# Weight gradients finished inside the second batch's tail, sums read from PSUM, and convolution gradients written as rows

## Chip, cores and metric

The kernel runs on one core of one Trainium2 chip. The metric is the device time of one execution in microseconds (us), as the median of several runs. Engines: PE is TensorE (matmul), PEld its weight load, DVE is VectorE, ACT is ScalarE, POOL is GpSimd, SP is SyncE; "SPq" and "ACTq" are DMA issues by SyncE and ScalarE.

## The reference, cut to what matters

The reference is the forward pass of one branch-merging encoder layer and all of its gradients, for 2 batches of 4000 tokens of width D = 144, in bfloat16. The kernel returns the output, the gradient of `x`, and seven weight gradients (out2 to out8). Convolutions have K = 5 taps.

```python
def _fwd_reference(x, w_qkv, w_att_out, w_mlp_in, dw_csgu, w_mlp_out, dw_merge, w_merge):
    xa = _layernorm(x)
    q, k, v = split(xa @ w_qkv)
    glob = softmax(q k^T * D**-0.5) v @ w_att_out
    u, g = split(gelu(layernorm(x) @ w_mlp_in)); g = _layernorm(g)
    gc = sum over i of shift(g, i) * dw_csgu[i]          # dw_csgu is (5, 144)
    m = concat(glob, (u * gc) @ w_mlp_out)
    m = m + sum over i of shift(m, i) * dw_merge[i]      # dw_merge is (5, 288)
    return x + m @ w_merge

def reference(*args, grad_out):                          # shortened
    out, vjp = jax.vjp(_fwd_reference, *args)
    return (out, *vjp(grad_out))
```

Weight gradients are sums over the tokens of both batches. out5 is the gradient of `dw_csgu` and out7 that of `dw_merge`: five rows each, with the channels along the row.

## The kernel before

For each batch the program runs a head, an attention phase and a *tail*. The tail walks over 32 token blocks in 16 half-steps plus 4, and gathers two sets of sums in PSUM: `EF` (correlations of activations with the shifted `grad_out`, 12 tiles of 144 columns) and, in the four last half-steps, `gr`. At the end of a tail both are spilled to DRAM:

```python
        def spill_ef():
            EFs = pp.tile([128, 12, D], F32, name="EFs")
            nc.gpsimd.memset(EFs[64:128, 10:12, :], 0.0)
            for n_ in range(3):
                nc.scalar.copy(EFs[:, n_ * 3:n_ * 3 + 3, :], EF[:, n_, 0:3 * D].rearrange("p (a b) -> p a b", b=D))
            # ... two more copies ...
            nc.sync.dma_start(k.A.EF_d[b][:], EFs[:])
        # spill_gr() does the same with gr, to k.A.gr_d[b]

            for h in range(NPR + 4):                  # NPR = 16
                # ... loads, turns, EF matmuls, dx matmuls of this half-step, cut ...
                if h == NPR:
                    spill_ef()
                # ...
                if 0 <= h - 4 < NPR:
                    out_mm(h - 4)                     # the output's matmuls
                if h >= NPR:
                    gr_part(range((h - NPR) * 8, (h - NPR) * 8 + 8))
                # ...
            spill_gr()
```

After both batches, `finish_weights` loads weights and both batches' sums, adds them, and works out the weight gradients:

```python
def finish_weights(k, W):
    # ...
        for name, (dr, shp) in W.fin.items():
            F[name] = fp.tile(shp, BF, name="f_" + name)
            nc.sync.dma_start(F[name][:], dr[:])
        # ...
        for t, dr, n in ((A.EF, A.EF_d, 12), (A.gr, A.gr_d, 4)):
            o = fp.tile([128, n, D], F32, name="f_o%d" % n)
            nc.sync.dma_start(t[:], dr[0][:])
            nc.sync.dma_start(o[:], dr[1][:])
            nc.vector.tensor_tensor(t[:], t[:], o[:], op=ALU.add)
        # ... ET, E80: the sums as bf16 ...
        for kk in range(5):                           # 16 partitions of each tap, to partition 0
            nc.sync.dma_start(ETr[0:DR, :, kk, :], E80[(4 - kk) * DR:(5 - kk) * DR, :, :])
        # dU: 8 PSUM tiles of matmul, 20 pairs of VectorE operations
        for h in range(2):
            for ct in range(2):
                for (k0, k1) in ((0, 3), (3, 5)):
                    # ... pt = WmT^T (ET, ETr) ...
                    for kk in range(k0, k1):
                        nc.vector.scalar_tensor_tensor(dU[0:cw, h, ct, :], pt[0:cw, kk - k0, :], W.wm[...], dU[0:cw, h, ct, :], op0=ALU.mult, op1=ALU.add)
                        nc.vector.scalar_tensor_tensor(jk[0:cw, :], pt[0:cw, kk - k0, :], 1.0, W.UT[h][0:cw, ct, :], op0=ALU.mult, op1=ALU.mult, accum_out=dwm[...])
        # the turn: ET and ETr transposed to Ej; dm: 20 VectorE operations, to out8
        # transposes and small products, to out2, out3, out4, out6
        # ...
        with nc.allow_non_contiguous_dma(reason="small conv weight gradients"):
            nc.sync.dma_start(k.out5[:, 0:128].rearrange("k c -> c k"), dwcb[:, 0, :])
            nc.sync.dma_start(k.out5[:, 128:D].rearrange("k c -> c k"), dwcb[112:128, 1, :])
            for h in range(2):
                nc.sync.dma_start(k.out7[:, h * D:h * D + 128].rearrange("k c -> c k"), dwmb[:, h, 0, :])
                nc.sync.dma_start(k.out7[:, h * D + 128:h * D + D].rearrange("k c -> c k"), dwmb[0:DR, h, 1, :])
```

In the program's text the writes of `dwcb` (out5) stand at the end. They depend on nothing late, so the scheduler moved them forward.

Of the kernel before, what the change touches and what calls it, by code (L numbers as in the profile page):

```python
# [10 lines left out]
ALU = mybir.AluOpType  # L11
# [1866 lines left out]
def phase_tail(k, W, b, S):  # L1878
# [3 lines left out]
    with ExitStack() as es:  # L1882
# [13 lines left out]
        EF = ps_e.tile([128, 4, 512], F32, tag="EF", name="EF")  # L1896
# [40 lines left out]
        def corr(g, j):  # L1937
            i = g * 4 + j
            for s in range(6):
                lhs = G["gs", g][:, j, s, 0:128] if s < 5 else G["g80", g][:, j, :]  # L1940
                mw = 128 if s < 5 else 80
                for h, mv in enumerate((S.Yn[:, i, :], G["ug", g][:, j, :])):
                    q = s * 2 + h
                    nc.tensor.matmul(EF[0:mw, q // 3, (q % 3) * D:(q % 3 + 1) * D], lhs, mv,
                                     start=(i == 0 and q % 3 == 0), stop=(i == NBK - 1), skip_group_check=True)
# [76 lines left out]
        def spill_ef():  # L2022
            EFs = pp.tile([128, 12, D], F32, name="EFs")
            nc.gpsimd.memset(EFs[64:128, 10:12, :], 0.0)
            for n_ in range(3):
                nc.scalar.copy(EFs[:, n_ * 3:n_ * 3 + 3, :], EF[:, n_, 0:3 * D].rearrange("p (a b) -> p a b", b=D))
            nc.scalar.copy(EFs[:, 9:10, :], EF[:, 3, 0:D].rearrange("p (a b) -> p a b", b=D))
            nc.scalar.copy(EFs[0:80, 10:12, :], EF[0:80, 3, D:3 * D].rearrange("p (a b) -> p a b", b=D))
            nc.sync.dma_start(k.A.EF_d[b][:], EFs[:])

        def gr_part(r):
            if r[0] == 0:
                st["gr"] = ps_e.tile([128, 4, 512], F32, tag="EF", name="gr")
            gr = st["gr"]
            for i in r:
                for n_, (p_, w) in enumerate(parts(i)):
                    nc.tensor.matmul(gr[0:w, n_ // 2, (n_ % 2) * D:(n_ % 2 + 1) * D], p_, S.xaa[:, i, :],  # L2037
                                     start=(i == 0 and n_ % 2 == 0), stop=(i == NBK - 1), skip_group_check=True)

        def spill_gr():  # L2040
            gr = st.pop("gr")
            grs = pp.tile([128, 4, D], F32, name="grs")
            nc.gpsimd.memset(grs[:, 3, :], 0.0)
            nc.scalar.copy(grs[:, 0:2, :], gr[:, 0, 0:2 * D].rearrange("p (a b) -> p a b", b=D))
            nc.scalar.copy(grs[:, 2, :], gr[:, 1, 0:D])
            nc.scalar.copy(grs[0:48, 3, :], gr[0:48, 1, D:2 * D])
            nc.sync.dma_start(k.A.gr_d[b][:], grs[:])

        NPR = NBK // 2
        with tc.manual_schedule():  # L2050
# [3 lines left out]
            prep(0)  # L2054
            for h in range(NPR + 4):
# [28 lines left out]
                if h >= NPR:  # L2084
                    gr_part(range((h - NPR) * 8, (h - NPR) * 8 + 8))
                if h < NPR:
# [8 lines left out]
def finish_weights(k, W):  # L2095
    nc, tc = k.nc, k.tc
    A = k.A
    c = float(D) ** -0.5
    with tc.tile_pool(name="fw", bufs=1) as fp, tc.tile_pool(name="fw_ps", bufs=3, space=PSUM) as ps:
        id_ = W.ident  # L2100
# [4 lines left out]
        W.WoT, W.UT, W.U, W.WmT, W.Wqkv = F["WoT"], [F["UT0"], F["UT1"]], [F["U0"], F["U1"]], F["WmT"], F["Wqkv"]  # L2105
        A.EF = fp.tile([128, 12, D], F32, name="f_EF")
        A.gr = fp.tile([128, 4, D], F32, name="f_gr")
        for t, dr, n in ((A.EF, A.EF_d, 12), (A.gr, A.gr_d, 4)):
            o = fp.tile([128, n, D], F32, name="f_o%d" % n)
            nc.sync.dma_start(t[:], dr[0][:])  # L2110
            nc.sync.dma_start(o[:], dr[1][:])
            nc.vector.tensor_tensor(t[:], t[:], o[:], op=ALU.add)

        ET = fp.tile([128, 2, 5, D], BF, name="f_ET")
        E80 = fp.tile([128, 2, D], BF, name="f_E80")
        for h in range(2):
            for kk in range(5):
                nc.vector.tensor_copy(ET[:, h, kk, :], A.EF[:, (4 - kk) * 2 + h, :])
            nc.scalar.copy(E80[0:80, h, :], A.EF[0:80, 10 + h, :])
        ETr = fp.tile([128, 2, 5, D], BF, name="f_ETr")  # L2120
        nc.gpsimd.memset(ETr[:], 0.0)
        for kk in range(5):
            nc.sync.dma_start(ETr[0:DR, :, kk, :], E80[(4 - kk) * DR:(5 - kk) * DR, :, :])
        dU = fp.tile([128, 2, 2, D], F32, name="f_dU")
        nc.vector.memset(dU[:], 0.0)
        dwm = fp.tile([128, 2, 2, 5], F32, name="f_dwm")
        nc.vector.memset(dwm[:], 0.0)
        jk = fp.tile([128, D], F32, name="f_jk")
        for h in range(2):
            for ct in range(2):  # L2130
                cw = 128 if ct == 0 else DR
                for (k0, k1) in ((0, 3), (3, 5)):
                    n = (k1 - k0) * D
                    pt = ps.tile([128, 3, D], F32, tag="H")
                    for kt, e_ in enumerate((ET, ETr)):
                        nc.tensor.matmul(pt[0:cw, 0:k1 - k0, :].rearrange("p a b -> p (a b)"), W.WmT[:, h, kt, ct * 128:ct * 128 + cw],  # L2136
                                         e_[:, h, k0:k1, :].rearrange("p a b -> p (a b)"), start=(kt == 0), stop=(kt == 1))
                    for kk in range(k0, k1):
                        nc.vector.scalar_tensor_tensor(dU[0:cw, h, ct, :], pt[0:cw, kk - k0, :], W.wm[0:cw, h, ct, kk:kk + 1], dU[0:cw, h, ct, :], op0=ALU.mult, op1=ALU.add)  # L2139
                        nc.vector.scalar_tensor_tensor(jk[0:cw, :], pt[0:cw, kk - k0, :], 1.0, W.UT[h][0:cw, ct, :], op0=ALU.mult, op1=ALU.mult, accum_out=dwm[0:cw, h, ct, kk:kk + 1])  # L2140

        for h in range(2):
            Ej = fp.tile([128, 2, 5, D], BF, name="f_Ej%d" % h)
            nc.gpsimd.memset(Ej[:, 1, :, :], 0.0)
            for kk in range(5):
                for jt_ in range(2):
                    jw = 128 if jt_ == 0 else DR
                    pt = ps.tile([128, D], BF, tag="T")
                    nc.tensor.transpose(pt[0:jw, 0:128], ET[:, h, kk, jt_ * 128:jt_ * 128 + jw], id_[:])  # L2149
                    nc.tensor.transpose(pt[0:jw, 128:D], ETr[0:DR, h, kk, jt_ * 128:jt_ * 128 + jw], id_[0:DR, 0:DR])  # L2150
                    nc.scalar.copy(Ej[0:jw, jt_, kk, :], pt[0:jw, :])
            for ct in range(2):
                cw = 128 if ct == 0 else DR
                dm = fp.tile([128, D], F32, name="f_dm%d%d" % (h, ct))
                nc.vector.memset(dm[:], 0.0)
                for (k0, k1) in ((0, 3), (3, 5)):
                    pt = ps.tile([128, 3, D], F32, tag="H")
                    for kt in range(2):
                        nc.tensor.matmul(pt[0:cw, 0:k1 - k0, :].rearrange("p a b -> p (a b)"), W.U[h][:, kt, ct * 128:ct * 128 + cw],  # L2159
                                         Ej[:, kt, k0:k1, :].rearrange("p a b -> p (a b)"), start=(kt == 0), stop=(kt == 1))  # L2160
                    for kk in range(k0, k1):
                        nc.vector.scalar_tensor_tensor(dm[0:cw, :], pt[0:cw, kk - k0, :], W.wm[0:cw, h, ct, kk:kk + 1], dm[0:cw, :], op0=ALU.mult, op1=ALU.add)  # L2162
                dmb = fp.tile([128, D], BF, name="f_dmb%d%d" % (h, ct))
                nc.vector.tensor_copy(dmb[0:cw, :], dm[0:cw, :])
                nc.sync.dma_start(k.out8[h * D + ct * 128:h * D + ct * 128 + cw, :], dmb[0:cw, :])

        def tr(src, R, C, name):

            nk, nck = (R + 127) // 128, (C + 127) // 128
            t = fp.tile([128, nck, R], BF, name=name)  # L2170
            nc.vector.memset(t[:], 0.0)
            for cc in range(nck):
                w = min(128, C - cc * 128)
                for kt in range(nk):
                    rk = min(128, R - kt * 128)
                    pt = ps.tile([128, D], BF, tag="T")
                    nc.tensor.transpose(pt[0:w, 0:rk], src[0:rk, kt, cc * 128:cc * 128 + w], id_[0:rk, 0:rk])
                    nc.vector.tensor_copy(t[0:w, cc, kt * 128:kt * 128 + rk], pt[0:w, 0:rk])
            return t

        def prod_out(lhs_k, rhs_k, rc0, scale, out_ap, name):
            for mt in range(2):
                mw = 128 if mt == 0 else DR
                pt = ps.tile([128, 3, D], F32, tag="H")
                for kt in range(2):
# [132 lines left out]
```

## Time and profile before

| | before |
|---|---|
| median, us | 1449.94 (3 runs, 1448.42 to 1453.59) |
| span of the profiled run, us | 1449.8 |
| start of the second tail, us | 1281.7 |
| first `gr` matmul of the second tail | 1361.8 |
| last `gr` matmul ends | 1374.6 |

The table of windows of the kernel before gives each engine's busy us in a stretch (number of instructions in brackets), then the granted TensorE clock, the DMA engines' busy share and GB/s:

```profile
core 0: us, PE busy (x) PEld busy (x) DVE busy (x) ACT busy (x) POOL busy (x), PEclk, DMA share, GB/s
1340.00:1350.00 10.00, 9.72 (x157) 9.54 (x157) 5.76 (x22) 5.59 (x15) 6.06 (x13) 1.00 0.72 185
...
1380.00:1390.00 10.00, 1.06 (x4) 0.32 (x4) 4.22 (x14) 0.52 (x2) 0.00 (x0) 0.50 0.68 243
1390.00:1400.00 10.00, 1.08 (x5) 0.46 (x5) 0.65 (x3) 0.29 (x2) 0.00 (x0) 0.50 0.02 4
1400.00:1410.00 10.00, 9.67 (x46) 4.10 (x45) 6.69 (x38) 4.86 (x19) 0.00 (x0) 0.50 0.01 2
```

From 1340 to 1350 us TensorE is busy 97% of the time (from 1350 to the last `gr` 89%). After the last `gr` the engines work in turns for 75 us, at half clock from 1380. From 1390 to 1400 us almost nothing works, and the DMA engines are idle too (share 0.02). The chain of waits of the kernel before (start, length, what) says why:

```profile
1379.03 6.89 DMA f_o<-EF_d
1386.02 1.97 DVE f_EF L2112
1388.01 0.53 ACT f_E L2119 x2
1388.60 10.72 DMA f_ETr<-f_E
1401.06 0.93 PE pt L2136 x2
...
1425.66 0.50 ACT f_dWk_o L2188 x2
```

The sums come back from DRAM (6.9 us), are added and cast, and then five copies of 9 KB each wait 10.7 us. The timeline of SyncE in the kernel before shows what stood ahead of them, and what was issued last:

```profile
1380.79 0.43 SPq L2226 DMA_DIRECT2D out_dram<-f_dwcb  x1
1381.27 0.54 SPq L2227 DMA_DIRECT2D out_dram<-f_dwcb  x1
1388.60 3.18 SPq L2123 DMA_DIRECT2D f_ETr<-f_E  x5
...
1429.27 0.42 SPq L2229 DMA_DIRECT2D out_dram<-f_dwmb  x1
1429.73 4.15 SPq L2230 DMA_DIRECT2D out_dram<-f_dwmb  x1
```

Its DMA issues (count, KB each, median us from issue to landing):

```profile
f_ETr<-f_E SPq DMA_DIRECT2D x5, 9.0 KB, 10.7
...
out_dram<-f_dwi SPq DMA_DIRECT2D x1, 72.0 KB, 1.6
...
out_dram<-f_dwmb SPq DMA_DIRECT2D x2, 1.2 KB, 16.7
```

A store of 72 KB in rows lands in 1.6 us; one of 1.2 KB in columns takes 16.7. Two such column writes (`f_dwcb`) were issued over 7 us ahead of the `f_ETr` copies, and the last ones (`f_dwmb`) end the program.

### The profile page before, as it was taken

The page shows a single profiled execution, that of the slowest core. Times are in us where ns is not written, and L with a number is a line of the kernel's source. Part 1 is how long each engine was busy: PE and PEld are TensorE (multiplying, and loading weights), DVE is VectorE, ACT ScalarE, POOL GpSimd, SP SyncE. Part 2 cuts the span into 40 slices and gives each one's busy share as a digit, 9 for nine tenths or more (in the row PEclk, how much of TensorE's full clock was granted, in tenths as well). Part 3 has the DMA queues.
Part 4 walks back from the last instruction along what each step waited for, and adds up shares of the span by engine and source line. Part 5 has one row for each costly group of instructions (what it writes and reads, how often), then busy time and mean ns, then how long its engine had stood idle before and what let it go on. Part 6 is the DMA issues. An engine that isn't in the chain of part 4 may idle for free. (4 is left out here: it accounts for less than half of the span.)

```text
span 1449.8 us, 40173 instructions
## 1 busy us (share of the span) xinstructions
PE 1289.7 (89%) x15366; PEld 981.9 (68%) x15366; DVE 933.5 (64%) x3213; ACT 807.8 (56%) x2377; POOL 544.5 (38%) x937
## 2 busy tenths in 40 slices
PE   5989999999999998899679999999999999979832
PEld 2727777777676776789553777777776777679811
DVE  5537778688677776355335778777767777636442
ACT  3746666666666754254365667666666665435310
POOL 2224435444434432355232343453434343245300
PEclk9969999999999999899896999999999999999955
DMA  4439999899999989756525999998987989966520
GB/s 135 121 60 158 162 169 173 152 187 160 163 167 163 164 176 175 169 164 171 177 76 102 156 183 143 177 176 148 186 168 148 160 149 192 176 158 187 138 84 13
DMA packets 652288, 220.65 MB, mean 152 GB/s; under 512 B 589876, under 2 KB 649012, under 8 KB 652084
## 3 DMA queue, kind: packets, MB, share of 16 engines
q1 hardware_dynamic: 651220, 217.89, 76.7%
q8 instruction: 122, 2.00, 0.6%
q14 instruction: 82, 0.67, 0.2%
q10 hardware_dynamic: 864, 0.09, 0.1%
HBM read 58.00 MB, written 25.13 MB: 57 GB/s over the span
## 5 line engine op out<-in xcount | busy, mean ns | idle before, releaser
L1778 DVE SCALAR_TENSOR_TENSOR Sm<-pD,Pm 128x500 bf16<-128x500 f32 x512 | 326.3, 675 | 226.6 <-ACT Pm L1777 185.4
L1777 ACT ACTIVATE Pm<-pS 128x500 bf16<-128x500 f32 x512 | 296.0, 585 | 110.6 <-PE pS L1772 107.0
L1831 PE MATMUL X<-Qs,Sm 128*128 128x144 bf16 x2048 | 293.6, 227 | 4.4 <-DVE acc L1842 4.4
L1832 PE MATMUL X<-Bt,Pm 128*128 128x144 bf16 x2048 | 293.7, 227 | 0.0
L1840 POOL TENSOR_TENSOR acc<-xs,acc 128x432 f32<-128x432 f32 x160 | 179.0, 1119 | 242.6 <-ACT xs L1839 242.2
L1832 PEld LDWEIGHTS <-Pm 128*128 128x128 bf16 x2048 | 201.3, 98 | 15.5 <-issue 5.2
L1831 PEld LDWEIGHTS <-Sm 128*128 128x128 bf16 x2048 | 201.5, 98 | 10.4 <-issue 0.3
L1839 ACT COPY xs<-X 128x432 f32<-128x432 f32 x160 | 83.1, 519 | 170.7 <-PE X L1832 166.6
L1772 PE MATMUL pS<-xaT,QTm 128*128 128x500 bf16 x512 | 160.6, 397 | 0.0
L1811 PE MATMUL y<-xaa,PT 128*128 128x144 bf16 x2048 | 149.4, 226 | 9.1 <-DVE B_t L1819 8.9
L1772 PE MATMUL pD<-xaT,BTm 128*128 128x500 bf16 x512 | 157.5, 390 | 0.0
L1811 PE MATMUL y<-xaa,ST 128*128 128x144 bf16 x2048 | 148.8, 226 | 0.0
L1811 PEld LDWEIGHTS <-PT 128*128 128x128 bf16 x2048 | 134.4, 98 | 19.8 <-issue 13.8
L1811 PEld LDWEIGHTS <-ST 128*128 128x128 bf16 x2048 | 133.3, 98 | 9.5
L1842 DVE TENSOR_TENSOR acc<-X,acc 128x432 f32<-128x432 f32 x192 | 110.6, 576 | 28.4 <-PE X L1832 28.0
L1768 PE MATMUL pD<-XR,QBr 16*128 16x500 bf16 x512 | 119.2, 393 | 4.6 <-DVE Sm L1778 4.2
L1800 POOL TENSOR_SCALAR nr<-nd,rl 128x1 f32<-128x1 f32 x64 | 22.6, 353 | 258.5 <-DVE nd L1794 258.5
L1768 PE MATMUL pS<-XR,QBr 16*128 16x500 bf16 x512 | 110.6, 395 | 1.7 <-ACT QBr L1755 1.4
L1777 ACT ACTIVATION_READ_ACCUMULATOR Pm<-pS 128x1 f32 x512 | 103.3, 202 | 0.0
L1772 PEld LDWEIGHTS <-BTm 128*128 128x128 bf16 x512 | 51.9, 101 | 64.3 <-issue 9.8
L1772 PEld LDWEIGHTS <-QTm 128*128 128x128 bf16 x512 | 29.3, 98 | 80.7 <-issue 80.7
L2008 POOL TENSOR_SCALAR cc<-xaa,n 128x144 f32<-128x144 bf16 x64 | 36.0, 570 | 70.0 <-DVE n L2005 56.7
(584 smaller groups left out, 2602.1 us busy)
## 6 DMA issues: line engine op xcount, KB each, us to landing
gs<-in_grad_out_dram SPq DMA_DIRECT2D x24, 720.0 KB
gtap<-gn_d SPq DMA_DIRECT2D x16, 720.0 KB
dh_d<-dh SPq DMA_DIRECT2D x32, 144.0 KB, 2.8
dhr<-dh_d SPq DMA_DIRECT2D x16, 288.0 KB, 4.1
gs<-in_grad_out_dram SPq DMA_DIRECT2D x8, 540.0 KB
xg<-in_x_dram SPq DMA_DIRECT2D x28, 144.0 KB, 4.2
dug_d<-dug SPq DMA_DIRECT2D x16, 144.0 KB, 1.8
gn_d<-gn_t SPq DMA_DIRECT2D x32, 72.0 KB, 2.9
```

Of the source, the lines that this page charges most:

```text
L1768: nc.tensor.matmul(o_[:, 0:SC], QBr[rr, bi, :], S.XR[rr, c2, 0:SC], start=True, stop=False)
L1772: nc.tensor.matmul(p_[h][:, 0:SC], w_[:, bi, :], S.xaT[:, c0 + h * SC:c0 + (h + 1) * SC], start=False, stop=True)
L1777: nc.scalar.activation(P[:, pb, c1:c1 + SC], pS[h][:, 0:SC], ACT.Exp, accum_out=ld8[:, 0, n:n + 1])
L1778: nc.vector.scalar_tensor_tensor(Sm[:, pb, c1:c1 + SC], pD[h][:, 0:SC], 1.0, P[:, pb, c1:c1 + SC], op0=ALU.mult, op1=ALU.mult, accum_out=l ...
L1800: nc.gpsimd.tensor_scalar(nr[:], nd[:], rl[:], 1.0, op0=ALU.mult, op1=ALU.mult)
L1811: nc.tensor.matmul(y[:, w, :], src[:, jj, :], S.xaa[:, j, :], start=(j == 0), stop=(j == NBK - 1))
L1831: nc.tensor.matmul(X[:, jj, :], Sm[:, i % NP, j * 128:(j + 1) * 128], Qs[:, i % 4, :], start=(kk == 0 and jj == 0), stop=False, skip_group ...
L1832: nc.tensor.matmul(X[:, jj, :], P[:, i % NP, j * 128:(j + 1) * 128], Bt[:, i % 4, :], start=False, stop=(kk == 1), skip_group_check=True)
L1839: nc.scalar.copy(xs[:, 0:nj, :], X[:, 0:nj, :])
L1840: nc.gpsimd.tensor_tensor(a_, xs[:, 0:nj, :], a_, op=ALU.add)
L1842: nc.vector.tensor_tensor(a_, X[:, 0:nj, :], a_, op=ALU.add)
L2008: nc.gpsimd.tensor_scalar(cc[:, q, :], S.xaa[:, 2 * p + q, :], n[:, 1, q:q + 1], n[:, 0, q:q + 1], op0=ALU.mult, op1=ALU.add)
```

## The change

It has four parts.

1. Weights and the first batch's sums are loaded at the start of the second tail, with the fills of the tiles that need zeros.
2. The second batch's sums are not spilled: VectorE adds them to the first batch's straight from PSUM. Four separate EF banks let `gr` start when two are free.
3. The arithmetic of the weight gradients is put in four *slots* in the four last half-steps, one behind each `gr_part`; the rest follows in `gr()`.
4. out5 and out7 are transposed on TensorE and leave as contiguous rows. Some small stores go out on ScalarE's queue.

```diff
-        EF = ps_e.tile([128, 4, 512], F32, tag="EF", name="EF")
+        EF = [ps_e.tile([128, 512], F32, tag="EF%d" % n, name="EF") for n in range(4)]
+        fin_ = Finish(k, W, es, ps_t, ps_e) if b else None
@@ spill_ef
+            if fin_:
+                return fin_.ef(EF)
@@ the tail's loop
             prep(0)
+            if fin_:
+                fin_.loads()
             for h in range(NPR + 4):
@@
                 if h >= NPR:
                     gr_part(range((h - NPR) * 8, (h - NPR) * 8 + 8))
+                    if fin_:
+                        fin_.step(h - NPR)
@@
-def finish_weights(k, W):
+class Finish:
+    def loads(self):
+        # ... weights, EF0, gr0 from DRAM ...
+        nc.gpsimd.memset(self.Wk32[:], 0.0)
+        nc.gpsimd.memset(self.ETr[:], 0.0)
+        for h in range(2):
+            nc.gpsimd.memset(self.Ej[h][:, 1, :, :], 0.0)
+        nc.gpsimd.memset(self.dU[:], 0.0)
+        nc.gpsimd.memset(self.dwm[:], 0.0)
+        nc.gpsimd.tensor_copy(dwcb[:], A.dwc[:])
+        pt = self.T()
+        nc.tensor.transpose(pt[0:10, 0:128], dwcb[:].rearrange("p a b -> p (a b)"), W.ident[:])
+        nc.scalar.copy(o[0:10, :], pt[0:10, 0:128])
+        nc.sync.dma_start(self.k.out5[:, 0:128], o[0:5, :])
+        nc.sync.dma_start(self.k.out5[:, 128:D], o[5:10, 112:128])
+    def ef(self, EF):
+        # ... five tensor_tensor adds ET = EF (PSUM) + EF0 ...
+        for m in range(5):
+            nc.sync.dma_start(self.ETr[0:DR, :, m, :], ET[m * DR:(m + 1) * DR, 10:12, :])
+    def step(self, n):
+        if n == 0:
+            self.turn(0)
+            self.turn(1)
+        elif n == 1:
+            self.dU_part(0, 0)
+            self.dU_part(0, 1)
+        elif n == 2:
+            self.dU_part(1, 0)
+            self.dU_part(1, 1)
+        else:
+            # ... dwm transposed, out7 as rows; out6, dWv, dWo ...
+    def gr(self, gr):
+        # ... gb = gr (PSUM) + gr0; dWq, dWk, out4 ...
+        for h in range(2):
+            for ct in range(2):
+                self.dm_part(h, ct)                   # out8
```

(All of it cut to its core; the computation of each gradient is the one of before.)

## The prediction

> **What bounds the kernel now.** Until 1374 us it is held by TensorE (table of windows: 1310 to 1350 us, PE 9.7 to 9.9 of 10 us busy). The change touches what follows: the last `gr` matmul starts at 1374.3 us (timeline), the span is 1449.8, so 75 us are a serial epilogue with granted clock 0.5 from 1380. The chain of waits and the timeline split it:
> - to 1386.0: SyncE issues loads, `f_o<-EF_d` lands.
> - to 1388.6: sum in SBUF (1.97 us), casts.
> - to 1399.3: `f_ETr<-f_E`, 10.7 us for five 9 KB copies. I blame the queue ahead: the element-wise `f_dwcb` writes were issued at 1380.8.
> - to 1426.2: arithmetic, mostly VectorE (20 `f_dU`/`f_jk` pairs of 0.50 us, 20 `f_dm` of 0.28).
> - to 1449.8: SyncE issues; the column write `f_dwmb` lands 16.7 us (DMA issues, median) after issue.
>
> The Trainium skill, "DMA: Bandwidth & Descriptors", Rules for kernel authors, says a non-contiguous last dim makes one descriptor per element; 16.7 us for 1.2 KB agrees.
>
> **What the change does.** Weights and batch-0 sums load at the start of the second tail; VectorE adds EF sums out of PSUM; the finishing is slotted into the four last half-steps; conv gradients are transposed on TensorE and leave as rows. TensorE keeps program order, so slotted pieces stall the `out_mm`/`gr` matmuls between them.
>
> My chain on the old clock (estimates from the durations above):
> - EF adds 0.6 us each; `gr` starts 1360.8 rather than 1361.8.
> - `turn` waits for the `ETr` copies (landing about 1366.5), then four 720-wide ScalarE copies of 0.9 us: TensorE free 1369.5.
> - Steps 1 and 2: `out_mm` 1.5 + `gr` 2.0 us, then 5 us of `dU` on VectorE each: 1385.5. Last `gr` 1387.
> - Step 3 and `gr()`: transposes, products, small DMA issues on ScalarE's queue: 1394.
> - `dm`, 20 x 0.28 us: 1400; last store lands: 1402.
>
> So 75 us become 28: −47.5.
>
> **Given back.**
> - Start of the second tail. TensorE's first tail instruction is now the `f_dwcb` transpose, behind GpSimd's `prep(0)` (ends 1285.7) and new memsets (`f_ETr` 1.3, `f_Ej` 2 x 0.7, others; 3.7 us). TensorE idles 1282.8 to 1289.5; before, it had done eight transposes and ten EF matmuls by then and waited 2.2 us. The tail is later TensorE-bound, so this passes through: +5.
> - That hole should drop the clock to 0.5 (at 1379 it dropped 4.7 us after the last matmul): +2.5.
> - Partly cold TensorE in the last half-steps: +3.
> - Batch 0: `gr` waits only for two of four EF banks: −1.
>
> 1450 − 47.5 + 5 + 2.5 + 3 − 1 ≈ 1411 us.
>
> **Predicted:** 1411 us, 8 in 10 between 1401 and 1424. Faster by over 2%: 0.85; within 2%: 0.14; slower: 0.01.
>
> **Right or wrong, in the profile.** From the last EF matmul to the end: before about 93 us, after 45 to 50. No DMA over 5 us in the last 30 us. `f_ETr` lands within 5 us of its first issue. A TensorE wait for GpSimd `f_dwcb` of 6 to 7 us at the tail's start, clock below 1 after it. The last chain is `f_dm`, then the `f_dmb` store. Phases up to 1282 us unchanged within 2 us.
>
> **What would make it wrong.** The early loads (1.8 MB) delaying tap loads of the second tail; a cold clock through 1365 to 1400 (+8); `ETr` still slow (+6); the start hole absorbed (−6).

## The result, and the profile after

| | before | after |
|---|---|---|
| median, us | 1449.6 (4 runs, 1448.42 to 1453.59) | 1410.64 (4 runs, 1409.07 to 1417.44) |
| span of the profiled run | 1449.8 | 1410.0 |
| start of the second tail | 1281.7 | 1277.9 |
| tail start to first `gr` | 80.1 | 83.0 |
| first `gr` to last `gr` | 12.7 | 28.5 |
| last `gr` to end | 75.2 | 20.6 |

The ratio is 0.9732, with a 95% interval of 0.97 to 0.9765. Ratios are the mean time of one kernel's fast runs over that of the other's fast runs of the same rounds, so they are not quite the ratio of the medians quoted. All ratios below are against the kernel before.

The start of the second tail, after; first GpSimd, then TensorE's first instruction there (the bracket: how long it sat idle, and what ended that):

```profile
1282.09 1.30 POOL L2126 MEMSET f_ETr<- 128x1440 bf16 x1
1283.33 1.34 POOL L2129 MEMSET f_Ej<- 128x720 bf16 x2
...
1285.19 0.19 POOL L2135 CAST f_dwcb<-A_dwc 128x10 bf16<-128x10 f32 x1
1285.43 0.27 PE L2137 MATMUL fT<-w_ident,f_dwcb 128*10 128x128 bf16 x1 [7.57 <-POOL f_dwcb L2135]
```

TensorE idles 7.57 us behind GpSimd, whose fills take the last 3.4 us of it (1281.9 to 1285.4), at the head of the phase that TensorE bounds. In place of the spill, the adds from PSUM and the copies of `f_ETr`, from the timelines of VectorE and SyncE:

```profile
1360.27 2.21 DVE L2155 TENSOR_TENSOR f_ET<-EF,f_EF 128x432 bf16<-128x432 f32 x5
1362.29 3.19 SPq L2158 DMA_DIRECT2D f_ETr<-f_ET  x5
```

The copies are there within 4.3 us of the first issue: TensorE's last wait for them ends at 1366.60. The windows after, with the same columns as before:

```profile
1282.00:1288.00 6.00, 2.57 (x22) 2.46 (x23) 0.43 (x1) 0.84 (x2) 3.38 (x7) 0.50 0.90 281
...
1364.00:1368.00 4.00, 1.81 (x18) 1.24 (x19) 0.65 (x2) 0.99 (x2) 1.14 (x4) 0.88 0.25 59
1368.00:1374.00 6.00, 6.00 (x59) 5.53 (x58) 0.46 (x1) 2.02 (x3) 0.00 (x0) 0.51 0.20 47
1374.00:1394.00 20.00, 15.09 (x177) 11.11 (x174) 12.21 (x66) 2.58 (x12) 0.00 (x0) 1.00 0.10 21
1394.00:1405.00 11.00, 6.76 (x20) 1.47 (x20) 7.86 (x24) 1.02 (x6) 0.00 (x0) 0.52 0.10 25
```

With each pause of TensorE comes a stretch at half clock: from within the wait for the fills (1281.7 to 1288.5), and after the wait for `f_ETr` (1367.0 to 1373.9). The end, from the timelines of VectorE and SyncE:

```profile
1396.04 0.37 DVE L2198 TENSOR_SCALAR f_dm<-fH,w_wm 128x144 f32<-128x144 f32 x1 [1.11 <-PE fH L2194]
1396.44 1.24 DVE L2200 SCALAR_TENSOR_TENSOR f_dm<-fH,w_wm,f_dm 128x144 f32<-128x144 f32 x3
...
1404.11 0.35 DVE L2200 SCALAR_TENSOR_TENSOR f_dmb<-fH,w_wm,f_dm 16x144 bf16<-16x144 f32 x1
1404.49 0.33 SPq L2202 DMA_DIRECT2D out_dram<-f_dmb  x1
```

The span ends 5.5 us after that last issue.

How steady are single profiles? The instruction order up to the second tail's start is the same in all variants of the changed kernel, yet that start fell anywhere from 1270.5 to 1280.9 us. So spans of single profiles differ by several us for no cause of their own, and the experiments are compared by stretches within the tail: from its start to the first `gr`, and from the first `gr` to the end. A control (below) gave 83.2 us for the first and 49.4 for the second, where the changed kernel has 83.0 and 49.1 (differences of rounded times: 0.1 us either way means nothing).

### The profile page after: what moved, and what is told of

Read it like the earlier page. It is cut to its first block, busy times and chain, and to the rows that moved or that the text cites. A ratio compares the mean times of both kernels' runs of the same rounds, so it can differ in the third digit from the quotient of the medians.

```text
span 1410.0 us, 40120 instructions
## 1 busy us (share of the span) xinstructions
PE 1282.5 (91%) x15366; PEld 981.2 (70%) x15366; DVE 932.7 (66%) x3182; ACT 802.3 (57%) x2354; POOL 541.2 (38%) x940
## 4 chain that ended last, share of the span: by engine, by line
PE 31%; DVE 7%; issue 5%; POOL 4%; ACT 2%; DMA 2%; SPq 0%; POOLq 0%; ACTq 0%; DVEq 0%
PE y L1811 7%; PE pS L1772 4%; PE X L1831 4%; PE X L1832 4%; PE pD L1772 3%; PE pS L1768 2%; DVE Sm L1778 2%; PE pc L1504 1%; POOL cc L2009 1%; PE pb L1421 1%; DMA gnC<-gnC_d 1%; PE pD L1768 1%; ACT Pm L1777 1%; POOL t L2010 1%; PE po L1969 1%
## 5 line engine op out<-in xcount | busy, mean ns | idle before, releaser
L1832 PEld LDWEIGHTS <-Pm 128*128 128x128 bf16 x2048 | 201.0, 98 | 15.3 <-issue 4.9
L1811 PEld LDWEIGHTS <-PT 128*128 128x128 bf16 x2048 | 134.6, 98 | 20.3 <-issue 14.3
L1842 DVE TENSOR_TENSOR acc<-X,acc 128x432 f32<-128x432 f32 x192 | 110.4, 575 | 28.5 <-PE X L1832 28.1
```

What stands on the lines that cost most here:

```text
L1811: nc.tensor.matmul(y[:, w, :], src[:, jj, :], S.xaa[:, j, :], start=(j == 0), stop=(j == NBK - 1))
L1832: nc.tensor.matmul(X[:, jj, :], P[:, i % NP, j * 128:(j + 1) * 128], Bt[:, i % 4, :], start=False, stop=(kk == 1), skip_group_check=True)
L1842: nc.vector.tensor_tensor(a_, X[:, 0:nj, :], a_, op=ALU.add)
```

## The experiments

Eleven kernels and a control were run, in three groups; all gave correct results. All medians are of fast runs. The kernel before, in the rounds of the three groups: 1449.45, 1451.08 and 1455.33 us.

| run | median, us | ratio to before | 95% | tail start to first `gr` | first `gr` to end |
|---|---|---|---|---|---|
| changed kernel | 1410.64 | 0.9732 | 0.97 to 0.9765 | 83.0 | 49.1 |
| c_after (control) | 1412.73 | 0.9712 | 0.9689 to 0.9736 | 83.2 | 49.4 |
| e1_rows | 1428.81 | 0.9858 | 0.98 to 0.9916 | 80.2 | 68.2 |
| e2_cols | 1424.13 | 0.9811 | 0.9761 to 0.9861 | 83.4 | 63.2 |
| e3_start | 1404.21 | 0.9674 | 0.9624 to 0.9723 | 78.4 | 49.5 |
| e4_serial | 1410.71 | 0.9724 | 0.9673 to 0.9775 | 83.6 | 50.5 |
| e5_dm | 1410.71 | 0.9726 | 0.9698 to 0.9754 | 83.9 | 46.9 |
| e6_warm | 1413.28 | 0.9742 | 0.9712 to 0.9772 | 84.5 | 50.3 |
| e7_fine | 1409.05 | 0.9719 | 0.969 to 0.9749 | 85.3 | 44.9 |
| e8_best | 1400.47 | 0.9651 | 0.9623 to 0.9679 | 81.4 | 38.6 |
| e9_cols_sp | 1423.72 | 0.9789 | 0.9761 to 0.9816 | 83.3 | 61.9 |
| e10_best | 1398.76 | 0.9611 | 0.9587 to 0.9636 | 79.5 | 38.4 |
| e11_warm16 | 1414.32 | 0.9727 | 0.9702 to 0.9751 | 83.7 | 48.5 |

The kernel before has 80.1 and 88.0 us in these two stretches. A ratio is known to about 0.003, which is 4 us, and in the first group (e1 to e4) only to 0.005 or 0.006, which is 7 to 8 us. A gain of 2 or 3 us in a stretch is therefore read from the stretches, and its effect on the whole time is left unproved.

### e1_rows: the kernel before, with part four of the change alone

```diff
+        pt = ps.tile([128, D], BF, tag="T")
+        nc.tensor.transpose(pt[0:10, 0:128], dwcb[:].rearrange("p a b -> p (a b)"), id_[:])
+        nc.scalar.copy(o[0:10, :], pt[0:10, 0:128])
+        nc.sync.dma_start(k.out5[:, 0:128], o[0:5, :])
+        nc.sync.dma_start(k.out5[:, 128:D], o[5:10, 112:128])
-            nc.sync.dma_start(k.out5[:, 0:128].rearrange("k c -> c k"), dwcb[:, 0, :])
-            nc.sync.dma_start(k.out5[:, 128:D].rearrange("k c -> c k"), dwcb[112:128, 1, :])
 # ... out7 in the same way, from a transpose of all 20 columns of dwmb
```

Expected:

> The kernel before, with only the conv gradients turned on TensorE and written as rows. My theory: the element-wise write of f_dwcb sits in the queue ahead of f_ETr, and the one of f_dwmb is the end of the span. So two waits go: f_ETr should land about 4 to 5 us after its first issue instead of 10.7 (it took 4.1 us in the changed kernel), and the last write about 2 us after its issue instead of 16.7. Together about -21 us: 1427 to 1431 us. Rival: f_ETr is slow by itself (small pieces, a chain of five issues): it stays near 10.7 us and only the last write is saved, about -14 us: 1434 to 1437 us.

Measured: 1428.81 us, 20.6 less than the kernel before in the same rounds (by the interval of the ratio, 12 to 29 less). From the last `gr` to the end takes 55.5 us rather than 75.2, which is 19.7 less. SyncE's timeline has the copies at the head of the queue and the last writes short:

```profile
1385.40 3.19 SPq L2123 DMA_DIRECT2D f_ETr<-f_E  x5
...
1417.26 1.83 SPq L2239 DMA_DIRECT2D out_dram<-f_dwmt  x4
```

TensorE's wait for `f_ETr` fell from 8.6 us to 0.5. What follows: about half of the change's gain of 39 us comes from the layout of two outputs of a few KB in all.

How do the column writes delay the copies? The records of single DMA packets and of the semaphores (both in the trace) show that it is not a queue of packets. In the kernel before, the column writes ran as 720 packets of 2 bytes, one for each element, and the last of them ended at 1387.4, before the first copy was issued. The copies' own packets had ended by 1393.3. What came late were the completions: a DMA is complete when its semaphore has got 16 increments, and those of the copies came until 1400.0, among those of the column writes (1387.5 to 1399.1). In e1 they came from 1387.1 to 1389.7, the first copy issued at 1385.4. The Trainium skill, "DMA: Bandwidth & Descriptors", section Queues, rings and completion order, says that a semaphore increment lands only after every earlier write from the same DMA engine; these two traces agree with it. Why the completion of a 2-byte write takes so long isn't shown.

### e2_cols: the changed kernel, with out7 by columns again

```diff
-            pt = self.T()
-            nc.tensor.transpose(pt[0:20, 0:128], dwmb[:].rearrange("p c h k -> p (c h k)"), W.ident[:])
-            # ... copy, four stores of rows
+                for h in range(2):
+                    nc.sync.dma_start(k.out7[:, h * D:h * D + 128].rearrange("k c -> c k"), dwmb[:, 0, h, :])
+                    nc.sync.dma_start(k.out7[:, h * D + 128:h * D + D].rearrange("k c -> c k"), dwmb[0:DR, 1, h, :])
```

Expected:

> The changed kernel, with only the write of the larger conv gradient (dw_merge) put back to columns. My theory: in the new order this write is issued at about 1389 us, 20 us before the end, so most of its 17 us pass beside the f_dm arithmetic; 1 to 5 us slower than the changed kernel: 1411 to 1416 us. Rival: rows are worth here what they are worth in the kernel before, about 14 us: 1424 us or more.

Measured: 1424.13 us, a miss for my theory and as the rival said. I had thought that the column write, issued 0.7 to 2.2 us after the last `gr`, would pass beside the `f_dm` arithmetic, since the changed kernel's last store leaves 15 us after the last `gr`. It doesn't. The waits view has

```profile
ACT f_dWq_o L2226 <- DMA out_dram<-f_dwmb: 13.5, 1, 13.5
```

ScalarE itself, which makes the copies out of PSUM there, stood for 13.5 us. The compiled program gives its DMAs eight completion semaphores in turn, shared by the issues of SyncE and ScalarE, and each issue first waits until the earlier DMA with that semaphore is complete; the wait of ScalarE is on the semaphore of the first column write. A slow write therefore stops whatever engine comes to issue a DMA eight places later. `f_dm` began 20.3 us after the last `gr` rather than 6.6. Run e9 tests this reading.

### e3_start: the changed kernel, with the fills spread over half-steps 2 to 8

```diff
-        nc.gpsimd.memset(self.ETr[:], 0.0)            # and the others, and the transpose of dwcb
+    def prelude(self, h):
+        if h == 2:
+            nc.gpsimd.memset(self.Wk32[:], 0.0)
+        elif h in (3, 4):
+            nc.gpsimd.memset(self.Ej[h - 3][:, 1, :, :], 0.0)
+        elif h in (5, 6):
+            nc.gpsimd.memset(self.ETr[:, h - 5], 0.0)
+        # h == 7: dU, dwm, dwcb; h == 8: transpose of dwcb, out5
```

Expected:

> The changed kernel, with the seven GpSimd fills and the transpose of the small conv gradient (dw_csgu) taken out of the start of the second tail and spread one by one over half-steps 2 to 8; the early loads stay. My theory: TensorE's wait of 7.6 us at the tail's start falls back to about 2 us, the tail runs 5 to 6 us less until its last half-steps, and 3 to 6 us of it reach the end: 1404 to 1408 us. Rival: the delay is absorbed later in the tail (a DMA wait for the r tiles at its end comes back in its place): within 1 us of 1410.

Measured: 1404.21 us. The stretch from the tail's start to the first `gr` is 78.4 us. It is 83.0 to 85.3 in the nine profiles with the fills at the start (mean 83.8), 78.4 to 81.4 in the three with the fills spread (mean 79.8), and 80.1 in the kernel before. The two others with the fills spread, e8 and e10, also add the EF sums in another order, and their first `gr` waits for that; so e3 is the fair one. Where the delay arises is seen at the first `cc` of GpSimd in the tail; in the kernel before, the changed kernel and e3 (tails that start at 1281.7, 1277.9 and 1270.5):

```profile
1291.31 0.92 POOL L2008 TENSOR_SCALAR cc<-xaa,n 128x144 f32<-128x144 bf16 x2 [5.60 <-issue]
```

```profile
1293.61 0.91 POOL L2009 TENSOR_SCALAR cc<-xaa,n 128x144 f32<-128x144 bf16 x2 [8.23 <-DVE n L2006]
```

```profile
1281.46 0.92 POOL L2009 TENSOR_SCALAR cc<-xaa,n 128x144 f32<-128x144 bf16 x2 [6.91 <-issue]
```

It comes 9.6, 15.7 and 11.0 us after the tail's start. From there to the first `gr` are 67.3 us in the changed kernel and 67.5 in e3. So the fills and the early transpose cost 4.7 us at the start, and all of it arrives at the first `gr`. The early loads, which stayed where they were in this run, cost nothing that shows: in e1, which has none, the first `cc` comes 11.1 us after the start.

### e4_serial: the changed kernel, with the four slots moved behind the loop

```diff
-                    if fin_:
-                        fin_.step(h - NPR)
@@
+            if fin_:
+                for n_ in range(4):
+                    fin_.step(n_)
             spill_gr()
```

Expected:

> The changed kernel, with the four slotted pieces moved out of the last half-steps and run after them, before the same ending. The intent of the change says that the slots hide the finishing behind the tail's matmuls; then taking them out costs about what they hold, 8 to 13 us: 1418 us or more. My theory: TensorE keeps program order and waits for VectorE inside each slot, so nearly nothing is hidden and the gain is of the removed DRAM trip and column writes alone: within 2 us of 1410; the gr matmuls end at about 1375 instead of 1389 us, without a cold clock in them.

Measured: 1410.71 us, ratio 0.9724: the same as with the slots. The stretch from the first `gr` to the end is 50.5 rather than 49.1 to 49.4 us. So "inside the tail" hides about 1 us. In program order TensorE meets the slot's matmuls, waits for VectorE to free PSUM, and only then goes on to the next `out_mm`.

### e5_dm: the changed kernel, with the dm sums of two column halves taken in turn

```diff
-            for m in range(m0, m1):
-                # dm = dm + pt[m] * w, five in a row, for one ct after the other
+            for m in range(m0, m1):
+                for ct in range(2):
+                    # dm[ct] = dm[ct] + pts[ct][m] * w          (four PSUM banks)
```

Expected:

> The changed kernel, with one edit in its last part: the f_dm sums of the two column halves are taken in turn (one step of each), with four PSUM banks, so that no VectorE operation reads what the one just before it wrote. Theory (the 0.40 us from one f_dm operation to the next, where I had predicted 0.28, is the cost of waiting for the result of the operation before it): the 20 operations come every 0.28 to 0.30 us, the part from the first to the last takes about 6 us rather than 8.4, and the time falls by 2 to 3 us against the changed kernel. Rival (0.40 us is what such an operation costs when it reads PSUM in this part): the part stays at 8 us or more and the time within 0.5 us.

Measured: the 20 operations took 6.1 us from first to last (1392.98 to 1399.11) rather than 8.4. VectorE's timeline of this run:

```profile
1394.09 1.72 DVE L2204 SCALAR_TENSOR_TENSOR f_dm<-fH,w_wm,f_dm 128x144 f32<-128x144 f32 x6
1395.74 0.62 DVE L2204 SCALAR_TENSOR_TENSOR f_dmb<-fH,w_wm,f_dm 128x144 bf16<-128x144 f32 x2
```

Six operations in 1.72 us, and the next starts 1.65 us after the first: one every 0.275 us. In the changed kernel three took 1.24 us, one every 0.40 us or so. Both kernels have the same operation, shapes and memories, but e5 also has four PSUM banks rather than two. That is a rival only for the operations that wait for a matmul: in the changed kernel these start 0.46 to 0.50 us after the one before, while those that wait on VectorE's own semaphore alone start 0.39 to 0.41 after it. By the data, that wait is for the operation just before in the changed kernel, and for the last but one in e5. Nor is it the reading of one bank twice in a row: in both kernels a `f_jk` reads the same PSUM tile as the `f_dU` just before it, doesn't need its result, and starts 0.28 us after it. The stretch from the first `gr` to the end fell by 2.2 to 2.5 us. The median, 1410.71, doesn't show it: the ratio of 0.9726 lies within what the changed kernel has. The theory of the 0.40 us stands; its worth in the whole time isn't shown.

### e6_warm and e11_warm16: dummy matmuls against the cold clock

```diff
+            ph = self.H()
+            nd = 16 if (h, jt) == (0, 0) else 4       # e11: 16 for the first, no others
+            for n in range(nd):
+                nc.tensor.matmul(ph[:].rearrange("p a b -> p (a b)"), id_[:], self.Wqkv[:, 0, :], start=(n == 0), stop=(n == nd - 1))
             for m in range(5):
                 nc.tensor.transpose(pt[0:jw, m, 128:D], self.ETr[0:DR, ...
```

Expected of e6:

> The changed kernel, with 28 dummy matmuls of 432 columns put in front of the transposes that wait for the f_ETr copies (16 before the first, 4 before each of the other three), their results unused. Theory (the pause for f_ETr costs twice, the second time because the clock falls to 0.5 until 1374 and the third out_mm and gr groups run at half speed): the granted clock stays at 0.9 or more through the 12 us after the first gr, the out_mm and gr groups right after take 1.5 and 2.0 us rather than 3.0 and 2.7, and the time falls by 1 to 3 us. Rival (VectorE's and ScalarE's work in the slots sets the pace, so a warm clock only makes TensorE wait longer): the clock is repaired and the time stays within 1 us.

Measured of e6: the clock stayed at 1.00 from the first `gr` to 1379, and `out_mm` and `gr` took 1.5 and 2.0 us, as the theory had it. But the 12 later dummies took 2.5 us of the chain themselves, and the stretch to the end grew to 50.3 us. This experiment was badly made, and e11 mends it.

Expected of e11:

> The sixth experiment with only the first 16 dummy matmuls, which run while TensorE waits for f_ETr, and none between the later groups, where the 12 others took 2.5 us of the chain themselves. Theory (the cold clock after the wait for f_ETr costs about 2 us of the third out_mm and gr groups): from the first gr to the first dU matmul takes 12.2 us or less rather than the 14.2 of the changed kernel, and the stretch from the first gr to the end 47 to 48 us rather than 49.1. Rival (the clock falls later instead, in the VectorE waits of the next slots, and nothing is won): that stretch stays within 0.7 us of the control's.

Measured of e11: from the first `gr` to the first dU matmul 11.9 us rather than 14.2, so the cold clock there does cost 2.3. But the stretch to the end is 48.5 us, only 0.6 to 0.9 less than in the changed kernel and the control, because the clock fell later. Windows of e11:

```profile
1366.00:1374.00 8.00, 7.53 (x101) 5.89 (x98) 0.81 (x3) 2.83 (x4) 0.00 (x0) 1.00 0.34 79
1374.00:1384.00 10.00, 6.32 (x73) 4.48 (x74) 8.37 (x50) 0.00 (x0) 0.00 (x0) 1.00 0.00 0
1384.00:1388.00 4.00, 4.00 (x41) 4.00 (x39) 2.75 (x15) 0.00 (x0) 0.00 (x0) 0.57 0.12 29
```

In the slots TensorE waits for VectorE (busy 6.3 of 10 us), the clock falls to 0.57 at 1384, and the saving is mostly given back. The rival is nearer: with an in-order TensorE that waits in every slot, a clock saved in one place is lost in another. The median of 1414.32 us shows no gain.

### e7_fine: the dU work in eight pieces, between out_mm and quarters of gr

```diff
+                n0 = (h - NPR - 1) * 3 if fin_ and h > NPR else 99
+                if n0 < 8:
+                    fin_.dU_piece(n0)
                 if 0 <= h - 4 < NPR:
                     out_mm(h - 4)
+                if n0 + 1 < 8:
+                    fin_.dU_piece(n0 + 1)
                 if h >= NPR:
-                    gr_part(range((h - NPR) * 8, (h - NPR) * 8 + 8))
+                    gr_part(range((h - NPR) * 8, (h - NPR) * 8 + 4))
+                    if n0 + 2 < 8:
+                        fin_.dU_piece(n0 + 2)
+                    gr_part(range((h - NPR) * 8 + 4, (h - NPR) * 8 + 8))
```

Expected:

> The changed kernel, with the dU work of the slots cut into its eight PSUM tiles and put between out_mm and quarters of gr, one tile between every two, rather than four at once in each of two slots. Theory (the slots hide little because TensorE keeps program order and stands through most of the 10 us of VectorE work): from the end of the turn to the last gr, 20 us before, takes 13 to 15, and the time falls by 5 to 7 us. Rival (TensorE and VectorE work in this stretch is slow for another reason, such as PSUM contention between the two or the cold clock): the stretch stays above 18 us and the time within 2 us.

Measured: from the end of the turn to the last `gr` 15.6 us rather than 19.9, and the stretch from the first `gr` to the end 44.9, which is 4.2 to 4.5 less. One window of e7, then one of the changed kernel, over the same work:

```profile
1370.00:1386.00 16.00, 15.93 (x188) 13.28 (x186) 12.63 (x67) 1.08 (x3) 0.00 (x0) 0.90 0.09 19
```

```profile
1370.00:1390.00 20.00, 16.10 (x186) 13.46 (x183) 12.38 (x67) 0.75 (x3) 0.00 (x0) 0.90 0.07 15
```

TensorE has the same 16 us of work in both. In e7 it is never idle; in the changed kernel it stands for 4 us. The theory holds, though the saving is smaller than the 5 to 7 us I expected: TensorE became the limit, and part of its work still ran on the cold clock. The median, 1409.05 us, again lies within the noise of the changed kernel's.

### e8_best and e10_best: all of it together

e8 takes the start of e3, adds the EF rows for `f_ETr` first and issues its copies from two engines, and orders the last four half-steps by a list (o: `out_mm`; g: `gr` blocks; p: dU pieces; t: turn; d: halves of dm; s: products of step three; c: casts):

```diff
+        SEQ = ("o12 g0-8 o13 p0 t0-0 g8-11 p1 t0-1 g11-14 p2",
+               "t1-0 g14-17 p3 t1-1 o14 p4 g17-22 p5",
+               "o15 p6 g22-25 p7 c d0-0 g25-28",
+               "d0-1 s0 d1-0 s1 d1-1 s2 g28-32")
```

Expected of e8:

> All that the experiments so far and the theories of this batch point to, in one kernel: the start of the second tail of the third experiment; the EF sums of the rows for f_ETr first and its five copies issued from two engines; the dU tiles, the turn, the dm sums (in turns of two) and step three's products put between out_mm and gr so that they run beside each other; only the gradients that need gr after the last gr. If the theories hold, the stretch from the start of the second tail to the end, 132 us in the changed kernel, takes 108 to 115, and the time is 1385 to 1394 us. If the gains only overlap each other, it stays at the 1404 of the third experiment or above.

Measured of e8: 1400.47 us, ratio 0.9651, clearly better than the changed kernel, but not the 1385 to 1394 I expected; from the tail's start to the end 120.0 us rather than 108 to 115. The last `gr` ended only 29.1 us after the first; as I read the trace, because dm and the transposes shared two PSUM banks and the engines waited for one another ahead of it. e10 puts `gr` first there and dm in the banks that `gr` leaves:

```diff
-               "o15 p6 g22-25 p7 c d0-0 g25-28",
-               "d0-1 s0 d1-0 s1 d1-1 s2 g28-32")
+               "o15 p6 g22-26 p7 c g26-32", "")
+        # and in gr(): sums of gr, d0-0, transposes, d0-1, dWq, dWk, s0, d1-0, s1, d1-1, s2
```

Expected of e10:

> The eighth experiment with another order at the end: the last gr matmuls directly after the last dU tile, and the f_dm sums, the products of step three and those of gr after it, between one another (f_dm in the two PSUM banks that gr leaves). Theory (in the eighth, TensorE, VectorE and ScalarE each waited for one another for 10 us before the last gr, because f_dm and the transposes shared two PSUM banks, and the gr products then came alone): from the first gr to the end takes 31 to 34 us rather than 38.6, and the time is 1392 to 1396 us. Rival (the late stores, the clock and the small operations on ScalarE set the end anyway): 37 us or more, 1399 to 1401.

Measured of e10: the last `gr` does end 18.7 us after the first, not 29.1. But the stretch to the end is 38.4 us, the same as in e8, and the median is 1398.76 us (ratio 0.9611). The rival holds. The work that e8 had done before its last `gr` now came after it, no faster. Two lines of the waits view of e10 show part of that:

```profile
DVE f_dm L2222 <- PE fD L2215: 3.2, 2, 2.6
...
ACT f_dWo_o L2252 <- DMA out_dram<-f_dWv_o: 1.2, 1, 1.2
```

VectorE waited 2.6 us for a dm matmul that stood in TensorE's order behind transposes, which in turn waited for ScalarE; and ScalarE waited again at the issue of a store. The last store was issued at 1392.4, 6.4 us before the end. In the same rounds e10 takes 14.0 us less than the control (1398.76 and 1412.73), and it is the fastest kernel of this study.

### e9_cols_sp: e2 with all finishing stores issued by SyncE

```diff
-            (nc.sync if mt == 0 else nc.scalar).dma_start(out_ap[mt * 128:mt * 128 + mw, :], o[0:mw, :])
+            nc.sync.dma_start(out_ap[mt * 128:mt * 128 + mw, :], o[0:mw, :])
 # and the stores of out4 and out6 alike
```

Expected:

> The second experiment again (the out7 gradient written by columns in the changed kernel), but with the finishing stores that ScalarE issued moved to SyncE. Theory (the column write cost 13.5 us there because ScalarE itself stood behind its own store issue, which waited for the slow write; not because the write ends late): ScalarE waits no longer, f_dm starts within 8 us of the last gr as in the changed kernel (there 6.6), and the time returns to 1409 to 1414 us. Rival (the slow write holds back the DMA engines, or the order of the writes on them, whoever issues): the late stores still land late, and the time stays at 1421 us or more.

Measured: 1423.72 us: the rival's number. Yet ScalarE no longer waited, and `f_dm` started 5.2 us after the last `gr` and ended at 1399.2, as my theory had it. The stores moved the wait with them. The waits view of SyncE's queue and its timeline:

```profile
SPq L2227 <- DMA out_dram<-f_dwmb: 14.5, 2, 10.8
```

```profile
1389.33 0.84 SPq L2227 DMA_DIRECT2D out_dram<-f_dWv_o  x2
1401.01 2.92 SPq L2227 DMA_DIRECT2D out_dram<-f_dWo_o  x2
1407.73 0.81 SPq L2227 DMA_DIRECT2D out_dram<-f_dWq_o  x2
...
1410.79 1.80 SPq L2202 DMA_DIRECT2D out_dram<-f_dmb  x4
```

The arithmetic was done at 1399.2, but its stores were issued only from 1410.8, because SyncE's queue stood 14.5 us on the completion of the column writes. So what e2 showed has two halves, and my theory saw one. The slow write blocks later issues, on either engine; on ScalarE that stops arithmetic as well, but the end comes equally late in both. The Trainium skill, "DMA: Bandwidth & Descriptors", section Issuing engines are not separate DMA queues, says that DMAs of different engines run on the same DMA engines and that spreading the issues only saves time on the issuing sequencer. This pair agrees: 1424.13 and 1423.72 us. The packet records tell which of the two is late. The 1440 packets of 2 bytes of the column writes ended by 1389.0 us, and from 1392 to 1401 no packet of data was recorded. But the four column writes were complete only at 1401.0, 1401.5, 1407.7 and 1407.9, and so was a store of rows issued behind them (`f_dl`, issued at 1388.4, complete at 1408.0). So the packets did not wait; the completions did, as in e1, and each later issue waited for one of them.

### c_after: the control

Expected:

> A control: the changed kernel itself, unedited, in the same rounds as the three others. It should repeat its 1410.6 us within 2 us, and its stretch from the first gr matmul of the second tail to the end, 49.1 us in its first profile, within 1 us. If that stretch moves by more, differences of 1 to 2 us read from single profiles say nothing.

Measured: 1412.73 us, 2.1 above the first, in rounds in which the kernel before was 5.7 us slower than in the first ones; ratios 0.9712 and 0.9732. The stretch from the first `gr` to the end: 49.4 and 49.1 us. So differences of 1 us and more in that stretch can be read from single profiles; ratios cannot show 2 us.

## Why the prediction was right or wrong

The time, 1411 predicted and 1410.64 measured, was right, but that it came so close is luck: the errors of the rows below, −2.8, −3.6, −0.9, +2.8 and +3.5 us, cancel to −1.0. The mechanisms named were mostly right; several sizes were not. Point by point:

| step of the prediction | predicted | measured |
|---|---|---|
| before the second tail (and batch 0) | −1 | −3.8 in this pair of profiles; the shared code ahead of the tail varies by more than that |
| start of the second tail to first `gr` (+5, +2.5, EF adds −1) | +6.5 | +2.9 (mean of nine profiles +3.7) |
| first `gr` to first `f_dm` (with +3 for the cold clock) | 36 | 35.1 |
| `f_dm`, 20 operations | 5.6 | 8.4 |
| last issue to the end | 2 | 5.5 |

- **What bounds the old ending: right, and shown.** The cause named for the 10.7 us of `f_ETr`, the column writes queued ahead, was only blamed in the prediction. e1 shows it: without them the wait is 0.5 us. The last column write as the end of the program is shown by the same run. The two together are 20.6 us. That the copies stand in a queue behind them is not what the traces show: it is their completions that come late.
- **The start of the tail: mechanism right, sizes off.** The wait of TensorE for `f_dwcb` was 7.57 us (predicted 6 to 7), and the clock was at 0.50 by its end. "The tail is later TensorE-bound, so this passes through: +5" was right: against e3 the fills cost 4.7 us at the first `cc`, and 4.6 arrive at the first `gr`. Mis-sized were the terms beside it. "+2.5" for the clock: in the changed kernel TensorE worked on the cold clock from 1285.4 to 1288.5, so it lost at most about 1.6 us (an estimate from these times); and e1 and e3, without the fills at the start, have a cold stretch of 3.4 us there too, so it is not the fills' alone. "−1" for the `gr` that waits for two of four EF banks: in the kernel before and in e1 the first `gr` waited 1.49 us for the copies of the spill, and that went. The rest of the difference lies in the one profile of before: TensorE waited there 1.0 us for a DMA (`r<-u`) near the tail's end, which the profiles of after and e1 don't have. That wait doesn't vanish because the tail is late: e7, whose tail is as late, has one of 1.4 us.
- **"20 x 0.28 us" for `f_dm`: the step that failed in the ending.** I took the pace from before, where the scheduler had mixed two chains. In the changed kernel each operation reads the result of the one before it: 0.40 us apart (up to 0.50 where it also waits for a matmul), 8.4 us in all. e5 shows that this is the cause. The Trainium skill, "VectorE: DVE Perf Modes", section The DRAIN you can't avoid, says that a semaphore after each operation costs nothing extra, because the next one waits for an empty pipeline anyway (and that one which is not held starts earlier). The page's test is with copies; in these runs it does cost: operations of 0.35 to 0.37 us each start 0.275 us apart when they wait for the last but one, 0.40 when they wait for the last.
- **"Last store lands: 1402", two us behind the last operation: mis-sized by 3.5.** It left out what lies between the last landing and the end of the span. It could have been read before: 1429.27 plus 16.7 is 1446.0, and the span ends at 1449.8. After, the last completion comes at 1406.3, 1.8 us after the last issue and 3.7 before the end. It isn't a constant: over the fourteen profiles it is 2.2 to 5.5 us.
- **The slots: "slotted pieces stall the matmuls between them" was right**, and more so than the change's intent has it: e4 shows that the four slots are worth about 1 us. The gain of the change comes from the rows (20.6 us by e1) and from what e1 still lacks (no trip through DRAM, loads done early, fewer operations; 18 us in all, the rest of the difference). No run takes these 18 us apart; most of it is probably the way to the `f_ETr` copies (not tested alone), the first of which is issued 15.3 us after the last `gr` in e1, and ahead of the last `gr` in e4. e7, e8 and e10 show that a finer order does hide work.
- **"The cold clock: +3": right in size (2.3 us by e11), but not a saving to be had**: kept warm there, it falls elsewhere. The Trainium skill, "TensorE: Matmul & The Clock Gate", section What's actually happening, gives half clock after an idle window of about 3.4 us, and full clock after a busy one. The traces agree on the length: every stretch in the clock's records that ends within the span is a multiple of 3.41 us, such as the 6.83 from 1367.0 to 1373.9 in the changed kernel. But the window need not be idle throughout: in the 3.41 us before this drop TensorE was busy for 1.1 us, and in those before the next one, at 1394.4, for 2.3.
- **Checks named in the prediction**: from the last EF matmul to the end "45 to 50" was 53.3 us (missed, by the last two terms above); `f_ETr` within 5 us was 4.3; the last chain is `f_dm` and its store, as said; no wait for a DMA of over 5 us is left in the last 30 us, as said. "Phases up to 1282 us unchanged within 2 us" missed at 3.8, and was a bad check, since that start varies by up to 10 us between profiles of like code.

## What to carry to other kernels

Two thousand elements written by columns cost about 20 us here, nearly as much as all of the arithmetic at the end of the program (27 us in the profile before): transpose them on TensorE first, and look in the DMA issues for small writes that take long and for what is issued behind them. Moving work into a busy loop hid only about 1 us here, where an in-order engine met it as a block; cut it so finely that each piece's wait is covered by other work of the same engine, and check with the serial version that the overlap is worth anything. When chaining durations for a prediction, ask of each pace whether the operations were independent where it was read, and add the time from the last landing to the end of the span.

## What the Trainium skill lacked or had wrong

- "VectorE: DVE Perf Modes", The DRAIN you can't avoid: it says that a semaphore after each operation costs nothing extra. It doesn't tell apart which earlier operation the next one waits for. Measured: operations on 144 f32 columns, 0.35 to 0.37 us each, start 0.275 us apart when each waits for the last but one (e5_dm), and 0.40 us apart when each waits for the last (changed kernel): 6.1 against 8.4 us for 20 of them.
- "DMA: Bandwidth & Descriptors", Rules for kernel authors: it says that a non-contiguous last dim makes one descriptor per element, but gives no time for a small write of this kind to memory. Measured: 16.7 us for 1.2 KB, where 72 KB in rows took 1.6. The packets of 2 bytes were soon done (720 of them by 1387.4 us in the kernel before); the completions, and those of the copies issued behind them, came until 1400.0.
- The same page, Issuing engines are not separate DMA queues: the page has it elsewhere that the issuing sequencer waits for semaphores before it dispatches a DMA, but not that ScalarE as the issuer then does no arithmetic either. Measured: ScalarE stood 13.5 us (e2_cols); SyncE's queue stood 14.5 us when it issued the same stores (e9_cols_sp).
- "TensorE: Matmul & The Clock Gate", which advises to keep TensorE warm: it lacks that, where TensorE waits in several places, repairing one may only move the cold stretch. Measured: 2.3 us won at the first place, 0.6 to 0.9 left at the end (e11_warm16).
- In none of the pages: a figure counted from the last store's landing to the end of the profiled span (that stages follow a kernel's own work is said, but their times aren't given from this point). Measured: 3.7 us before and after, 2.2 to 5.5 over all profiles.
